# Attention with normalised queries and keys, then a bilinear FFN: queues ordered by a list, weights rounded in place, sums over keys by TensorE for 12 pairs

## The chip, the cores and the metric

The kernel runs on one core of a Trainium2 chip. The metric is the device time of one execution in microseconds, from the start of the program to its end; a span is the time from the first to the last instruction that the profiler recorded.

## The reference

Queries, keys and values are float32, of shape (8 batches, 12 heads, 448, 64). The weights of the FFN are float64: `w_a` and `w_b` 768 x 1536, `w_out` 1536 x 768.

```python
def rmsnorm(x, g):
    rms = np.sqrt(np.mean(x * x, axis=-1, keepdims=True) + 1e-06)
    return x / rms * g
q_n, k_n = (rmsnorm(q, g_q), rmsnorm(k, g_k))
scores = 1.0 / np.sqrt(64) * np.matmul(q_n, k_n.transpose(0, 1, 3, 2))
attn = np.exp(scores - np.max(scores, axis=-1, keepdims=True))
attn = attn / (np.sum(attn, axis=-1, keepdims=True) + 1e-09)
x = np.matmul(attn, v).transpose(0, 2, 1, 3).reshape(3584, 768)
out = ((x @ w_a) * (x @ w_b)) @ w_out
```

## The kernel before

All three rounded weights stay in SBUF. The work has three parts, which the program interleaves on in-order queues.

**Attention** goes by pairs of heads, 48 of them, six to a batch. `load` (line 149) brings a pair's queries, keys and values into two buffers each. `normalize` (164) squares q and k on POOL (172), sums on VectorE (173), raises the means to -0.5 with a power on POOL (176), and scales q on VectorE (179); the keys' scale goes into the exponential later. `transpose_qk` (185) makes eight transposes on TensorE into one PSUM tile and copies the halves out, k by ScalarE (197) and q with the gains by VectorE (198). `scores` (202) handles one of four key chunks of 112 for both heads: two products (207), two exponentials on ScalarE (211). `add_up` (213) adds the four chunks' exponentials, the first two on VectorE (217), then two additions of 112 x 896 on POOL (219). `values` (221) multiplies with v (227). `put_out` (256) copies the result into `xT`, the FFN's input, and `divide` (265) sums over the partitions with a product by ones that spreads the sum to 64 partitions per head (`su`, 270), takes a reciprocal of 128 x 448 (272) and multiplies `xT` (275). A pair's key sums thus use VectorE, POOL and TensorE in turn.

**Weights.** The float64 weights come in 72 units of 128 x 384: 48 of `w_a` and `w_b` in turn, by groups of 384 columns, then 24 of `w_out`. `load_weights` (115) brings a unit's words into one of two staging tiles (`raw`, low and high words side by side). `round_weights` (122) makes float32 of them: ScalarE (138) takes the high word's magnitude into `mag`, VectorE works in four steps (139 to 142), ScalarE scales the low word into `low` (143), and POOL multiplies and adds (144, 145). `mag` and `low` have one buffer each.

**The FFN** goes by eight blocks of 384 or 512 tokens (`ffn`, 277). The first stage has 12 column groups of 128; each takes six products with `w_a` and six with `w_b` into one of two PSUM tiles (`pf`, 285); ScalarE copies the first into `hT` (288), VectorE multiplies the second in (290). The second stage multiplies `hT` with `w_out` (`po`, 298) in two halves of 384 columns for each 128 tokens, copies out by VectorE or ScalarE (303, 305) and stores.

**The order** of the queues is the order in which the code issues. The main loop (344 to 382) goes by half pairs; `ffn` is a generator, and `some` (322) draws from it in proportion to the time of its products, so that a block's products are spread evenly over the six pairs of the next batch. Units are rounded one per half pair for the first 12 and six per half pair after that, all at one place of the loop (377 to 381). After the last pair the last block runs alone.

Of the kernel before, what the change touches and what calls it, by code (L numbers as in the profile page):

```python
# [22 lines left out]
ABOVE, BELOW = _float_of(0x47F00000), _float_of(0x38000000)  # L23


@with_exitstack
def kernel(
# [25 lines left out]
    nc = tc.nc  # L53
# [58 lines left out]
    def fast_body(ld, wk, ps_s, ps_o, ps_mm):  # L112
        raws = {}

        def load_weights(n):
            if n < len(units):
                src, dst, kc, c = units[n]
                raws[n] = ld.tile([P, WC, 2], U32, tag="stage", name="raw")
                nc.sync.dma_start(raws[n].rearrange("p n w -> p (n w)"),
                                  src[kc * P:(kc + 1) * P, 2 * c * WC:2 * (c + 1) * WC])  # L120

        def round_weights(n):

            if n >= len(units):
                return
            src, dst, kc, c = units[n]  # L130
            raw = raws.pop(n)
            lo, hi = raw[:, :, 0], raw[:, :, 1]
            w = dst[:, kc, c * WC:(c + 1) * WC]
            wb = w.bitcast(U32)
# [12 lines left out]
        qs, ks, vs, rs, qns, qkTs = {}, {}, {}, {}, {}, {}  # L147

        def load(p, what):
            if p >= NP:  # L150
                return
            b, h0 = p // HP, 2 * (p % HP)
            for held, src, nm in ((qs, q, "q"), (ks, k, "k"), (vs, v, "v")):
                if nm not in what:
                    continue
                if nm == "k":
                    held[p] = ld.tile([SP, NJ, 2, D], FP32, tag=nm, name=nm + "_sb")
                    for e in range(2):
                        nc.sync.dma_start(held[p][:, :, e], src[b, h0 + e].rearrange("(p j) d -> p j d", j=NJ))
                else:  # L160
                    held[p] = ld.tile([SP, 2, NJ * D], FP32, tag=nm, name=nm + "_sb")
                    nc.sync.dma_start(held[p], src[b, h0:h0 + 2].rearrange("h (p j) d -> p h (j d)", j=NJ))

        def normalize(p):

            if p >= NP:
                return
            ms = wk.tile([SP, 2, 2 * NJ], FP32, tag="ms", name="ms", bufs=3)
            for s, x in enumerate((qs[p], ks[p])):
                sq = wk.tile([SP, 2 * NJ, D], FP32, tag="sq", name="sq")  # L170
                flat = x.rearrange("p h (j d) -> p (h j) d", d=D) if s == 0 else x.rearrange("p j h d -> p (j h) d")
                nc.gpsimd.tensor_tensor(sq, flat, flat, ALU.mult)  # L172
                nc.vector.tensor_reduce(ms[:, s], sq, AX, ALU.add)  # L173
# [326 lines left out]
```

## Time and profile before

| | |
|---|---|
| median of 3 runs | 2007.9 us (2006.7 to 2008.88) |
| the profiled execution, its own time | 2006.51 us |
| its span | 2004.6 us |
| TensorE (PE) busy | 1769.9 us, 88% |
| VectorE (DVE), ScalarE (ACT), POOL busy | 594.9, 404.9 and 590.6 us |
| mean granted TensorE clock | 0.946 |

Busy time is the time in which an engine had an instruction running; PE is products, PEld the loading of stationary operands, which overlaps them. A granted clock of 1.00 is 2.4 GHz, 0.50 is 1.2 GHz. A float32 product leaves two records in the trace, a transpose one. The idle time of a row is that of the engine just ahead of its instructions, with what ended it. The rows are named by the line of the kernel and by tiles: `sc` scores, `ET` exponentials, `o` values' result, `pt` and `qkT` transposes and their copies, `ms` the means and the power, `su` and `sum` key sums, `pf` and `po` the FFN's two stages.

### The profile page before, as it was taken

The numbers are of one execution on the slowest core, as the hardware profiler recorded it, in microseconds if no ns is written. First come the engines' busy times: TensorE is split into PE (matmuls) and PEld (weight loads), VectorE is DVE, ScalarE is ACT, GpSimd is POOL, SyncE is SP. The second block draws the span as 40 slices with busy tenths as digits, with TensorE's granted clock in tenths as the row PEclk, the third lists the DMA queues.
The fourth block names the chain that finished last, engine by engine and source line by source line (L and its number), as shares of the span: only waits on it lengthen the run. The fifth ranks groups of instructions, "written<-read, shape, count | busy, mean of one in ns | idle before, by whom it ended". The sixth has DMA issues, their size and how long they took to land.

```text
span 2004.6 us, 15250 instructions
## 1 busy us (share of the span) xinstructions
PE 1769.9 (88%) x5760; PEld 851.6 (42%) x5760; DVE 594.9 (30%) x824; ACT 404.9 (20%) x773; POOL 590.6 (29%) x396
## 2 busy tenths in 40 slices
PE   4642455649999999999999999999999999999998
PEld 1211232324444455555444455554444555554445
DVE  4766544443223212232222122323222213210000
ACT  3423222322211112211121112121121112200000
POOL 5665544453212212322222123223212322200000
PEclk9885777779999999999999999999999999999999
DMA  3323223230100011001000111011010111000000
GB/s 90 80 66 102 80 76 92 78 93 22 39 19 14 18 34 36 25 17 44 22 14 14 39 34 28 14 35 30 14 28 14 30 30 28 5 16 8 0 6 27
DMA packets 87318, 73.43 MB, mean 37 GB/s; under 512 B 49348, under 2 KB 78020, under 8 KB 87236
## 3 DMA queue, kind: packets, MB, share of 16 engines
q1 hardware_dynamic: 87236, 72.38, 13.1%
q8 instruction: 47, 0.77, 0.2%
q14 instruction: 35, 0.29, 0.1%
HBM read 61.34 MB, written 11.01 MB: 36 GB/s over the span
## 4 chain that ended last, share of the span: by engine, by line
PE 80%; DVE 9%; POOL 7%; ACT 2%; issue 1%; SPq 0%; DMA 0%; POOLq 0%; DVEq 0%; ACTq 0%
PE pf L285 42%; PE po L298 22%; PE sc L207 6%; PE o L227 6%; POOL low L144 3%; PE su L270 2%; DVE mag L139 2%; POOL ms L176 2%; DVE sum L272 1%; POOL sum L219 1%; DVE mag L140 1%; ACT mag L138 1%; DVE mag L142 1%; PE pt L196 1%; PE pt L193 1%
## 5 line engine op out<-in xcount | busy, mean ns | idle before, releaser
L285 PE MATMUL pf<-xT,w_b_sb 128*128 128x512 f32 (+1 forms) x1152 | 460.4, 550 | 58.5 <-DVE hT L290 39.6
L285 PE MATMUL pf<-xT,w_a_sb 128*128 128x512 f32 (+1 forms) x1152 | 461.8, 551 | 43.1 <-ACT hT L288 43.1
L298 PE MATMUL po<-w_out_sb,hT 128*128 128x384 f32 x1344 | 446.7, 489 | 0.0
L285 PEld LDWEIGHTS pf<-xT,w_b_sb 128*128 128x128 f32 x1152 | 216.9, 192 | 294.7 <-issue 167.2
L298 PEld LDWEIGHTS po<-w_out_sb,hT 128*128 128x128 f32 x1344 | 251.2, 190 | 191.9 <-issue 28.4
L285 PEld LDWEIGHTS pf<-xT,w_a_sb 128*128 128x128 f32 x1152 | 218.8, 194 | 261.6 <-issue 152.6
L172 POOL TENSOR_TENSOR sq<-k_sb 112x512 f32<-112x512 f32 x48 | 49.9, 1040 | 852.7 <-DVE ms L173 852.7
L211 ACT ACTIVATE ET<-sc,ms 112x448 f32<-112x448 f32 x384 | 212.4, 637 | 243.8 <-PE sc L207 240.9
L219 POOL TENSOR_TENSOR sum<-sum,ET 112x896 f32<-112x896 f32 x96 | 200.0, 2084 | 130.4 <-ACT ET L211 79.2
L272 DVE RECIPROCAL sum<-su 128x448 f32<-128x448 f32 x48 | 141.9, 2957 | 270.8 <-PE su L270 270.8
L290 DVE TENSOR_TENSOR hT<-hT,pf 128x384 f32<-128x384 f32 (+1 forms) x96 | 59.4, 619 | 513.4 <-PE pf L285 513.0
L227 PE MATMUL o<-ET,v_sb 112*64 112x448 f32 x768 | 180.8, 594 | 19.2 <-ACT ET L211 19.2
L207 PE MATMUL sc<-qkT 64*112 64x448 f32 x768 | 173.6, 571 | 1.3 <-DVE qkT L198 1.3
L176 POOL TENSOR_TENSOR ms<-ms,expo 112x16 f32<-112x16 f32 x48 | 139.7, 2911 | 48.4 <-DVE ms L175 48.4
L288 ACT COPY hT<-pf 128x384 f32<-128x384 f32 (+1 forms) x96 | 51.1, 532 | 498.2 <-PE pf L285 498.2
L144 POOL TENSOR_TENSOR low<-low,mag 128x384 f32<-128x384 f32 x72 | 76.9, 1069 | 132.9 <-DVE mag L142 110.9
L207 PEld LDWEIGHTS sc<-qkT 64*112 64x112 f32 x768 | 62.6, 177 | 114.8 <-issue 103.1
L227 PEld LDWEIGHTS o<-ET,v_sb 112*64 112x64 f32 x768 | 50.6, 144 | 124.6 <-issue 98.7
L303 DVE COPY o_sb<-po 128x384 f32<-128x384 f32 x28 | 15.6, 557 | 228.6 <-PE po L298 228.6
L173 DVE TENSOR_REDUCE ms<-sq 112x8 f32<-112x512 f32 x96 | 65.5, 682 | 56.5 <-POOL sq L172 56.5
L138 ACT ACTIVATE mag<-raw 128x384 f32<-128x384 f32 x72 | 39.8, 553 | 192.4 <-POOL low L144 192.4
L179 DVE TENSOR_TENSOR qn<-q_sb,ms 112x512 f32<-112x512 f32 x48 | 34.0, 709 | 145.1 <-POOL ms L176 145.1
(42 smaller groups left out, 689.2 us busy)
## 6 DMA issues: line engine op xcount, KB each, us to landing
q_sb<-in_q_dram SPq DMA_DIRECT2D x48, 224.0 KB, 3.1
k_sb<-in_k_dram SPq DMA_DIRECT2D x96, 112.0 KB, 3.2
v_sb<-in_v_dram SPq DMA_DIRECT2D x48, 224.0 KB, 3.0
raw<-in_moe_w_a_dram SPq DMA_DIRECT2D x24, 384.0 KB, 3.2
raw<-in_moe_w_b_dram SPq DMA_DIRECT2D x24, 384.0 KB, 3.2
raw<-in_moe_w_out_dram SPq DMA_DIRECT2D x24, 384.0 KB, 3.0
out_dram<-o_sb SPq DMA_DIRECT2D x16, 168.0 KB, 2.1
out_dram<-o_sb SPq DMA_DIRECT2D x16, 144.0 KB, 2.0
```

The source lines that it names most:

```text
L138: nc.scalar.activation(magf, hi.bitcast(FP32), AF.Abs)
L144: nc.gpsimd.tensor_tensor(low, low, magf, ALU.mult)
L173: nc.vector.tensor_reduce(ms[:, s], sq, AX, ALU.add)
L176: nc.gpsimd.tensor_tensor(msf, msf, expo, ALU.pow)
L207: nc.tensor.matmul(sc[:, e, 0:S], lhsT=kT[rows, c * SP:(c + 1) * SP], rhs=qT[rows, :], start=True, stop=True)
L211: nc.scalar.activation(E[:, e], sc[:, e, 0:S], AF.Exp, scale=rs[p][:, 1, 2 * c + e:2 * c + e + 1])
L219: nc.gpsimd.tensor_tensor(sums[p][0:SP], sums[p][0:SP], ETs[p, c], ALU.add)
L227: nc.tensor.matmul(os_[p][e * D:(e + 1) * D, :], lhsT=vs[p][:, e, c * D:(c + 1) * D], rhs=E[:, e], start=(c == 0), stop=(c == NJ - 1))
L272: nc.vector.reciprocal(rinv, su)
L285: nc.tensor.matmul(pf[:, 0:N], lhsT=w_sb[:, c, m * P:(m + 1) * P], rhs=xT[:, c, 0:N], start=(c == 0), stop=(c == KA - 1))
L290: nc.vector.tensor_tensor(hT[:, m, 0:N], hT[:, m, 0:N], pf[:, 0:N], ALU.mult)
L298: nc.tensor.matmul(po[:, 0:HALF], lhsT=hT[:, m, t * P:(t + 1) * P], rhs=w_out_sb[:, m, hs], start=(m == 0), stop=(m == KO - 1))
```

## The change

**A planner.** Nothing is issued while the code walks the work. Each operation is put into a list with its engine, an assumed time, a key and the names of what it reads and writes, rings of buffers included (`Plan.op`, `Plan.slot`). `Plan.run` then goes through the list as a schedule at build time: at each step it takes the engine that can start first, and on it, among the operations ready at nearly the same time, the one of the smallest key. A chain of TensorE operations is kept together, and a change of TensorE's tiling costs 0.18 in it. The order so found is issued. A pair's operations have its number as key, a unit n/4 + 1, FFN products 10,000 and more, evacuations -1. FFN products are cut into groups of three (first stage) and six (second stage).

**Weights.** The rounding works in the weight's own place in place of `mag` and `low`, and in the staged words: the fourth VectorE step writes over the high words, the low word's product over the low words. The 48 units of `w_a` and `w_b` are staged in the twelve rows of `w_out`, whose own units come last and use two staging tiles as before. In every third unit one VectorE step replaces ScalarE's scaling and POOL's product.

**Pairs 0 to 11** (`LEAD`) sum over keys on TensorE alone: 32 products of a 112 x 112 piece of exponentials with one column of ones give the sums by query; VectorE inverts 112 x 8 numbers; eight products with the identity bring them to the layout of `xT`. VectorE's and POOL's additions are gone for these pairs. Their squares go from POOL to ScalarE, and the scaling of q's transposes from VectorE to ScalarE. Later pairs keep the old way, with the reciprocal written into PSUM. Squares now go k before q.

```diff
+class Plan:
...
+    def op(self, engine, us, key, emit, reads=(), writes=(), mode=None, chain=None, kb=0):
...
+        while any(cands.values()):
+            best = None
+            for e, cs in cands.items():
+                if not cs:
+                    continue
+                f = free.get(e, 0.0) if e else 0.0
+                at = {}
+                for n in cs:
+                    turn = self.TURN if ops[n][5] != modes.get(e) else 0.0
+                    at[n] = max(f, ready[n]) + turn
+                t = min(at.values())
+                n = min((n for n in cs if at[n] <= t + (0.2 if e == "PE" else 0.05)), key=lambda n: (ops[n][2], n))
+                if best is None or at[n] < best[0]:
+                    best = at[n], e, n
+            t, e, n = best
+            cands[e].remove(n)
+            for x in links.get(ops[n][6], [n]) if ops[n][6] is not None else [n]:
+                if ops[x][5] != modes.get(e) and x != n:
+                    t += self.TURN
+                modes[e] = ops[x][5]
+                order.append((t, x))
+                t += ops[x][1]
...
+                if ops[x][7]:
+                    dma = max(dma, t) + ops[x][7] / 200.0
+                    end[x] = dma + 2.5
...
+        self.times = order, end
+        for _, n in order:
+            if ops[n][3] is not None:
+                ops[n][3]()
...
+        LEAD = 12
...
+        def weights(n):
...
+            src, dst, kc, c = units[n]
+            key = n / 4 + 1.0
+            w = dst[:, kc, c * WC:(c + 1) * WC]
+            wb, hold = w.bitcast(U32), {}
+            if dst is w_out_sb:
+                st, name = slot("stage", 2), f"out.{kc}"
+            else:
+                st, name = f"out.{n % KO}", f"{'a' if dst is w_a_sb else 'b'}.{c}.{kc}"
...
+            def load():
+                if dst is w_out_sb:
+                    raw = ld.tile([P, WC, 2], U32, tag="stage", name="raw")
+                else:
+                    raw = w_out_sb[:, n % KO].bitcast(U32).rearrange("p (n w) -> p n w", w=2)
+                hold["lo"], hold["hi"] = raw[:, :, 0], raw[:, :, 1]
...
-            mag = wk.tile([P, WC], U32, tag="mag", name="mag")
-            low = wk.tile([P, WC], FP32, tag="low", name="low")
-            magf = mag.bitcast(FP32)
-            nc.scalar.activation(magf, hi.bitcast(FP32), AF.Abs)
-            nc.vector.tensor_scalar(magf, magf, BELOW, ABOVE, ALU.max, ALU.min)
-            nc.vector.tensor_scalar(mag, mag, 3, 0x3FFFFFFF, ALU.logical_shift_left, ALU.bitwise_and)
-            nc.vector.scalar_tensor_tensor(wb, hi, 0xC0000000, mag, ALU.bitwise_and, ALU.bitwise_or)
-            nc.vector.tensor_scalar(mag, wb, 0xFF800000, None, ALU.bitwise_and)
-            nc.scalar.activation(low, lo, AF.Copy, scale=2.0 ** -52)
-            nc.gpsimd.tensor_tensor(low, low, magf, ALU.mult)
-            nc.gpsimd.tensor_tensor(w, w, low, ALU.add)
...
+            op("SP", 0.1, key - 2.0, load, writes=[st], kb=384)
+            op("ACT", 0.55, key, lambda: nc.scalar.activation(w, hif(), AF.Abs), [st], [name])
+            op("DVE", 0.4, key, lambda: nc.vector.tensor_scalar(w, w, BELOW, ABOVE, ALU.max, ALU.min), [], [name])
+            op("DVE", 0.4, key, lambda: nc.vector.tensor_scalar(
+                wb, wb, 3, 0x3FFFFFFF, ALU.logical_shift_left, ALU.bitwise_and), [], [name])
+            op("DVE", 0.56, key, lambda: nc.vector.scalar_tensor_tensor(
+                wb, hold["hi"], 0xC0000000, wb, ALU.bitwise_and, ALU.bitwise_or), [st], [name])
+            op("DVE", 0.56, key, lambda: nc.vector.tensor_scalar(
+                hold["hi"], wb, 0xFF800000, None, ALU.bitwise_and), [name], [st])
+            if n % 3 == 0:
+                op("DVE", 0.56, key, lambda: nc.vector.scalar_tensor_tensor(
+                    lof(), hold["lo"], 2.0 ** -52, hif(), ALU.mult, ALU.mult), [], [st])
+            else:
+                op("ACT", 0.55, key, lambda: nc.scalar.activation(lof(), hold["lo"], AF.Copy, scale=2.0 ** -52), [], [st])
+                op("POOL", 1.05, key, lambda: nc.gpsimd.tensor_tensor(lof(), lof(), hif(), ALU.mult), [], [st])
+            op("POOL", 1.05, key, lambda: nc.gpsimd.tensor_tensor(w, w, lof(), ALU.add), [st], [name])
...
+                    if p < LEAD:
+                        nc.scalar.activation(t, flat, AF.Square)
+                    else:
+                        nc.gpsimd.tensor_tensor(t, flat, flat, ALU.mult)
...
+                if p < LEAD:
+                    nc.scalar.activation(qkTs[p][:, 0], x, AF.Copy, scale=gain[:, 0:1])
+                else:
+                    nc.vector.tensor_scalar_mul(qkTs[p][:, 0], x, gain[:, 0:1])
...
+            def by_query():
+                sus[p] = ps_o.tile([P, S], FP32, tag="su", name="su")
+                for e in range(2):
+                    for j in range(NJ):
+                        for c in range(NJ):
+                            nc.tensor.matmul(sus[p][0:SP, e * NJ + j:e * NJ + j + 1],
+                                             lhsT=ETs[p, c][:, e, j * SP:(j + 1) * SP], rhs=ones[:, 0:1],
+                                             start=(c == 0), stop=(c == NJ - 1))
...
+                rs["inv", p] = wk.tile([SP, 2 * NJ], FP32, tag="inv", name="inv", bufs=2)
+                nc.vector.reciprocal(rs["inv", p], sus[p][0:SP, 0:2 * NJ])
...
+            def to_features():
+                for e in range(2):
+                    for j in range(NJ):
+                        n = e * NJ + j
+                        nc.tensor.matmul(sus[p][e * D:(e + 1) * D, j * SP:(j + 1) * SP],
+                                         lhsT=rs["inv", p][:, n:n + 1].to_broadcast([SP, D]),
+                                         rhs=ident[0:SP, 0:SP], start=True, stop=True)
+            if p < LEAD:
+                inv = slot("inv", 2)
+                op("PE", 3.2, p, by_query, [names["ET", p, c] for c in range(NJ)], [su], mode="full", chain=chains[0])
+                op("DVE", 0.2, p - 1, invert_few, [su], [inv])
+                op("PE", 0.9, p, to_features, [inv], [su], mode="cols", chain=chains[1])
+            else:
+                op("PE", 0.76, p, spread, [names["sum", p]], [su], mode="cols", chain=chains[1])
+                op("DVE", 3.0, p, invert, [], [su])
...
+                        def products(m=m, n=n, w_sb=w_sb, part=part, cs=cs):
+                            if part == 0:
+                                pfs[m, n] = ps_mm.tile([P, 512], FP32, tag="mm", name="pf")
+                            for c in cs:
+                                nc.tensor.matmul(pfs[m, n][:, 0:N], lhsT=w_sb[:, c, m * P:(m + 1) * P],
+                                                 rhs=xTs[b][:, c, 0:N], start=(c == 0), stop=(c == KA - 1))
+                        op("PE", len(cs) * N / 600, key, products,
+                           [f"{names['xT', b]}.{c}" for c in range(KA)] + [f"{w}.{m * P // WC}.{c}" for c in cs],
+                           [mm], mode="full")
...
+        for n in range(len(units)):
+            weights(n)
...
+                    loads(p, nm)
+                normalize(p)
+                transposes(p)
+            if p > 0:
+                values(p - 1, 2, f"A{p}")
+                values(p - 1, 3, f"A{p}")
+                if p - 1 < LEAD:
+                    sums_over_keys(p - 1, (f"A{p}", f"B{p}"))
...
+            if p > 0:
+                if p - 1 >= LEAD:
+                    sums_over_keys(p - 1, (f"A{p}", f"B{p}"))
+                put_out(p - 1)
...
+            if p >= 2 * HP and p % HP == 0:
+                ffn(p // HP - 2)
+        ffn(B - 1)
...
-            load(1, "qk")
-            for n in range(2):
-                load_weights(n)
-            normalize(0)
-            transpose_qk(0)
-            todo, loaded = 0, 2
-            for i in range(NH + LAG):
-                p, h = divmod(i, 2)
...
-                if h == 0:
...
-                        divide(p - 1)
...
-                upto = i + 1 if i < 12 else 12 + (i - 11) * 6
-                while todo < min(upto, len(units)):
-                    load_weights(loaded)
-                    loaded += 1
-                    round_weights(todo)
-                    todo += 1
...
+            plan.run()
```

**How instructions move.** *TensorE, one pair in the first batch.* Before, from the transposes of pair 1 to its scores:

```order
L193 MATMUL pt<-ident,k_sb 128x112 x4
L196 MATMUL pt<-ident,qn 128x112 x4
L227 MATMUL o<-ET,v_sb 64x448 x4
L207 MATMUL sc<-qkT 112x448 x4
L270 MATMUL su<-sum,ones 64x448 x2
L227 MATMUL o<-ET,v_sb 64x448 x4
L207 MATMUL sc<-qkT 112x448 x4
```

and now, from the transposes of pair 2:

```order
L331 MATMUL pt<-ident,k_sb 128x112 x4
L331 MATMUL pt<-ident,qn 128x112 x4
L376 MATMUL o<-ET,v_sb 64x448 x4
L416 MATMUL su<-ones,ET 112x1 x32
L357 MATMUL sc<-qkT 112x448 x4
L428 MATMUL su<-ident,inv 64x112 x8
L376 MATMUL o<-ET,v_sb 64x448 x4
L357 MATMUL sc<-qkT 112x448 x4
```

The spread sum of two products became 32 products ahead of the next pair's scores (`su<-ones,ET`) and eight behind them (`su<-ident,inv`), and the inverse on VectorE now lies between these two.

*VectorE around the first evacuation into hT.* Before (30 units of weights stand ahead of it):

```order
L139 TENSOR_SCALAR mag<-mag 128x384
L140 TENSOR_SCALAR mag<-mag 128x384
L141 SCALAR_TENSOR_TENSOR w_b_sb<-raw,mag 128x384
L142 TENSOR_SCALAR mag<-w_b_sb 128x384
L217 TENSOR_TENSOR sum<-ET 112x896
L290 TENSOR_TENSOR hT<-hT,pf 128x384
L198 TENSOR_SCALAR qkT<-pt,gain 128x448
L139 TENSOR_SCALAR mag<-mag 128x384
L140 TENSOR_SCALAR mag<-mag 128x384
```

and now (49 stand ahead of it):

```order
L242 TENSOR_SCALAR w_out_sb<-w_out_sb 128x384
L243 TENSOR_SCALAR w_out_sb<-w_out_sb 128x384
L245 SCALAR_TENSOR_TENSOR w_out_sb<-raw,w_out_sb 128x384
L247 TENSOR_SCALAR raw<-w_out_sb 128x384
L250 SCALAR_TENSOR_TENSOR raw<-raw 128x384
L521 TENSOR_TENSOR hT<-hT,pf 128x384
L314 TENSOR_TENSOR qn<-q_sb,ms 112x2x4x64
L242 TENSOR_SCALAR w_out_sb<-w_out_sb 128x384
```

The evacuation moved behind all of `w_a` and `w_b`, and the inverse of pair 7 follows behind 50 units; the units are no longer in blocks of six.

*TensorE in a second stage of the FFN.* Before:

```order
L196 MATMUL pt<-ident,qn 128x112 x4
L298 MATMUL po<-w_out_sb,hT 128x384 x12
L227 MATMUL o<-ET,v_sb 64x448 x4
L207 MATMUL sc<-qkT 112x448 x4
L298 MATMUL po<-w_out_sb,hT 128x384 x12
L270 MATMUL su<-sum,ones 64x448 x2
L298 MATMUL po<-w_out_sb,hT 128x384 x12
L227 MATMUL o<-ET,v_sb 64x448 x4
L207 MATMUL sc<-qkT 112x448 x4
L298 MATMUL po<-w_out_sb,hT 128x384 x12
```

and now:

```order
L534 MATMUL po<-w_out_sb,hT 128x384 x6
L406 MATMUL su<-sum,ones 64x448 x2
L376 MATMUL o<-ET,v_sb 64x448 x4
L357 MATMUL sc<-qkT 112x448 x4
L534 MATMUL po<-w_out_sb,hT 128x384 x6
L331 MATMUL pt<-ident,k_sb 128x112 x4
L331 MATMUL pt<-ident,qn 128x112 x4
L534 MATMUL po<-w_out_sb,hT 128x384 x6
L376 MATMUL o<-ET,v_sb 64x448 x4
L357 MATMUL sc<-qkT 112x448 x4
```

A pair's pieces moved from 12 second-stage products apart to six, in the second stage and in the first groups of the next block; the rest of a first stage runs without pairs between.

## Rows read from the trace of the kernel before

**Rows 1.** Stretches: busy us (instructions) per engine, clock, DMA share, GB/s.
```profile
0.00:100.00 100.00, 56.15 (x209) 20.59 (x210) 61.87 (x78) 36.72 (x71) 62.01 (x48) 0.86 0.31 85
100.00:466.00 366.00, 181.03 (x596) 86.91 (x596) 195.10 (x328) 108.56 (x209) 198.26 (x166) 0.74 0.30 80
466.00:1900.00 1434.00, 1434.00 (x4681) 691.66 (x4680) 332.99 (x411) 255.35 (x487) 330.33 (x183) 1.00 0.09 24
```

**Rows 2.** Timeline: start us, us, engine, line, operation. VectorE, then TensorE.
```profile
15.48 1.52 DVE L179 TENSOR_TENSOR qn<-q_sb,ms 112x512 f32<-112x512 f32 x1 [3.03 <-POOL ms L176]
...
466.08 8.01 PE L298 MATMUL po<-w_out_sb,hT 128*128 128x384 f32 x24
```

**Rows 3.** TensorE's waits, 20 to 460 us: us in total, times, longest.
```profile
PE pf L285 <- ACT hT L288: 62.0, 5, 18.9
...
PE pf L285 <- DVE hT L290: 39.6, 2, 19.8
...
PE su L270 <- POOL sum L219: 17.2, 7, 3.3
```

**Rows 4.** Timeline, 204 to 213 us: one weight unit, and the next one's start.
```profile
208.02 0.55 ACT L138 ACTIVATE mag<-raw 128x384 f32<-128x384 f32 x1 [10.51 <-POOL low L144]
208.06 0.99 POOL L145 TENSOR_TENSOR w_a_sb<-w_a_sb,low 128x384 f32<-128x384 f32 x1
208.60 0.67 DVE L139 TENSOR_SCALAR mag<-mag 128x384 f32<-128x384 f32 x1 [1.76 <-ACT mag L138]
...
209.31 0.36 DVE L140 TENSOR_SCALAR mag<-mag 128x384 uint32<-128x384 uint32 x1
209.70 0.56 DVE L141 SCALAR_TENSOR_TENSOR w_b_sb<-raw,mag 128x384 uint32<-128x384 uint32 x1
210.29 0.36 DVE L142 TENSOR_SCALAR mag<-w_b_sb 128x384 uint32<-128x384 uint32 x1
...
211.82 0.55 ACT L138 ACTIVATE mag<-raw 128x384 f32<-128x384 f32 x1 [2.19 <-POOL low L144]
```

**Rows 5.** Timeline, 45 to 56 us: VectorE and POOL at the same time.
```profile
50.45 4.34 POOL L219 TENSOR_TENSOR sum<-sum,ET 112x896 f32<-112x896 f32 x2
...
50.75 2.12 DVE L140 TENSOR_SCALAR mag<-mag 128x384 uint32<-128x384 uint32 x1
...
52.90 2.31 DVE L141 SCALAR_TENSOR_TENSOR w_b_sb<-raw,mag 128x384 uint32<-128x384 uint32 x1
```

**Rows 6.** TensorE's groups by shape, 500 to 1900 us: busy us, mean ns, idle.
```profile
L298 PE MATMUL po<-w_out_sb,hT 128*128 128x384 f32 x1076 | 359.0, 490 | 0.0
...
L285 PE MATMUL pf<-xT,w_b_sb 128*128 128x384 f32 x432 | 147.7, 492 | 0.0
L207 PE MATMUL sc<-qkT 64*112 64x448 f32 x560 | 123.3, 559 | 0.0
L227 PE MATMUL o<-ET,v_sb 112*64 112x448 f32 x568 | 122.4, 552 | 0.0
...
L193 PE MATMUL pt<-ident,k_sb 112*128 112x112 f32 x140 | 19.2, 259 | 0.0
```

**Rows 7.** Timeline around 702 us: eight transposes, and what follows them.
```profile
701.65 0.55 PE L193 MATMUL pt<-ident,k_sb 112*128 112x112 f32 x4
...
702.42 7.92 PE L298 MATMUL po<-w_out_sb,hT 128*128 128x384 f32 x24
```

**Rows 8.** Line 207, 160 to 200 us: duration in ns, min/median/max.
```profile
L207 PEld LDWEIGHTS sc<-qkT x16: 169/173/308, 172.1 to 199.7; 64*112 64x112 f32 x16
```

**Rows 9.** Stretches as in rows 1: clock and TensorE's busy time.
```profile
48.00:52.00 4.00, 4.00 (x12) 1.28 (x10) 3.08 (x4) 1.60 (x4) 3.92 (x3) 0.50 0.32 98
```

**Rows 10.** The fullest stretch; two groups of the page.
```profile
36.00:40.00 4.00, 4.00 (x16) 1.20 (x12) 3.90 (x4) 1.28 (x3) 2.54 (x3) 0.64 0.99 265
...
L211 ACT ACTIVATE ET<-sc,ms 112x448 f32<-112x448 f32 x384 | 212.4, 637 | 243.8 <-PE sc L207 240.9
...
L176 POOL TENSOR_TENSOR ms<-ms,expo 112x16 f32<-112x16 f32 x48 | 139.7, 2911 | 48.4 <-DVE ms L175 48.4
```

More of the change, by code (lines that the diff above doesn't have):

```diff
@@ L152, in load, with loads, emit @@
+        xs, rs, qns, qkTs, pts, scs, ETs, sums, sus, os_, xTs, tails = ({} for _ in range(12))
+        names = {}
+        def loads(p, nm):
             b, h0 = p // HP, 2 * (p % HP)
-            for held, src, nm in ((qs, q, "q"), (ks, k, "k"), (vs, v, "v")):
-                if nm not in what:
-                    continue
+            src = {"q": q, "k": k, "v": v}[nm]
+            names[nm, p] = slot(nm, 2)
+            def emit():
                 if nm == "k":
-                    held[p] = ld.tile([SP, NJ, 2, D], FP32, tag=nm, name=nm + "_sb")
+                    x = ld.tile([SP, NJ, 2, D], FP32, tag=nm, name=nm + "_sb")
@@ L164, in normalize @@
+                    nc.sync.dma_start(x, src[b, h0:h0 + 2].rearrange("h (p j) d -> p h (j d)", j=NJ))
+                xs[nm, p] = x
+            op("SP", 0.15, p - 2.0, emit, writes=[names[nm, p]], kb=230)
         def normalize(p):
[L166 to L173, printed above, removed]
@@ L200, in fast_body @@
-        ETs, sums, os_, xTs, tails = {}, {}, {}, {}, {}
-        def scores(p, c):
-            qT, kT = qkTs[p][:, 0], qkTs[p][:, 1]
-            sc = ps_s.tile([SP, 2, 512], FP32, tag="sc", name="sc")
-            for e in range(2):
-                rows = slice(e * D, (e + 1) * D)
-                nc.tensor.matmul(sc[:, e, 0:S], lhsT=kT[rows, c * SP:(c + 1) * SP], rhs=qT[rows, :],
-                                 start=True, stop=True)
-            E = ETs[p, c] = wk.tile([SP, 2, S], FP32, tag="ET", name="ET", bufs=4)
-            for e in range(2):
-                nc.scalar.activation(E[:, e], sc[:, e, 0:S], AF.Exp, scale=rs[p][:, 1, 2 * c + e:2 * c + e + 1])
+            ms = names["ms", p] = slot("ms", 3)
@@ new lines, in values, with product @@
+        def values(p, c, chain):
+            if c == 0:
+                names["o", p] = slot("o", 1)
+            def product():
+                if c == 0:
+                    os_[p] = ps_o.tile([P, S], FP32, tag="o", name="o")
+                for e in range(2):
+                    nc.tensor.matmul(os_[p][e * D:(e + 1) * D, :], lhsT=xs["v", p][:, e, c * D:(c + 1) * D],
+                                     rhs=ETs[p, c][:, e], start=(c == 0), stop=(c == NJ - 1))
+            op("PE", 0.76, p, product, [names["ET", p, c], names["v", p]], [names["o", p]], mode="cols", chain=chain)
@@ L233, in fast_body, with emit @@
-        ends = []
-        for b in range(B):
-            ends.append((b + 1) * S // P * P)
+                names["sum", p] = slot("sum", 1)
+            def emit():
+                if c == 1:
+                    sums[p] = wk.tile([P, 2, S], FP32, tag="sum", name="sum")
+                    nc.vector.tensor_tensor(sums[p][0:SP], ETs[p, 0], ETs[p, 1], ALU.add)
+                else:
+                    nc.gpsimd.tensor_tensor(sums[p][0:SP], sums[p][0:SP], ETs[p, c], ALU.add)
+            E = names["ET", p, c]
@@ L316, in store @@
                 rows = out[bb * S:(bb + 1) * S].rearrange("(p j) d -> j p d", j=NJ)
-                nc.sync.dma_start(rows[j][p0:p0 + n, hs], o_sb[at:at + n])
+                nc.sync.dma_start(rows[j][p0:p0 + n, h * HALF:(h + 1) * HALF], o_sb[at:at + n])
                 g, at = g + n, at + n
-        fill, due, done = None, 0.0, 0.0
-        def some(share):
-            nonlocal fill, due, done
-            due += share
-            while fill is not None and done < due:
-                took = next(fill, None)
-                if took is None:
-                    fill = None
-                else:
-                    done += took
@@ L383, in fast_body @@
-            some(1e9)
-            fill, due, done = ffn(B - 1), 0.0, 0.0
-            some(1e9)
+            plan.run()
+        return plan
     def general():
```

360 lines of the change are left out of this document (220 added, 140 removed).

## The prediction

> **What bounds the kernel now.** I read the table of stretches first. It splits the run in two: up to 466 us TensorE is busy 56.15 of 100 and 181.03 of 366 us, at a mean granted clock of 0.86 and 0.74; from 466 to 1900 us it is busy 1434.00 of 1434.00 us at 1.00 [rows 1]. The cut is where TensorE issues its first product with the third weight, at 466.08 us [rows 2]. So whatever the change does, the time can come only from ahead of that point, and what follows it is 2004.6 - 466.1 = 1538.5 us of work that waits for nothing.
>
> Then the waits of TensorE ahead of that point: the first FFN block waits 62.0 us for ScalarE and 39.6 us for VectorE to take its results out of PSUM [rows 3]. Neither engine is short of time (VectorE is busy 195 of 366 us [rows 1]); they are waiting in order behind weight rounding. One unit is a chain, ScalarE at 208.02, VectorE from 208.60 to 210.65, then POOL, and the next unit's ScalarE step starts at 211.82, since it reuses the one `mag` tile: 3.80 us a unit [rows 4]. Six units stand between two hT evacuations. This chain is what the change goes at.
>
> **The sum.** Time = T0 + what TensorE does after its first third-weight product + 1.9 us (the profiled execution took 2006.51 us for a span of 2004.6; the median of the runs shown is 2007.9, 1.4 us more). T0 is 466.1 us before.
>
> **After T0.** At that point the new queue has issued 108 score, 104 value and 112 transpose products against 96, 92 and 96 before. Products count two records each, transposes one. A record is a group's busy time over its count [rows 6]: 24 x 0.220 + 24 x 0.2155 + 16 x 0.137 = 12.6 us; since neighbours overlap, the ten groups of that stretch add up to 1449 us in 1400, 3.5% too much, so 12.2 us. What remains is 1538.5 - 12.2 = 1526 us. The later order I cost at nothing: a pair's pieces are now 12 third-weight records (12 x 0.334 = 4.0 us) apart instead of 24, and that covers the hop that each piece waits for, the two exponentials of a chunk (2 x 0.64 us [rows 10]). POOL's two additions of 2.17 us [rows 5] have three such gaps. If the cover fails it is the spread sum that is late; that is a rival below.
>
> **T0, first part: to the reciprocal of pair 7.** On VectorE the first hT evacuation now stands behind 49 units, and the reciprocal of pair 7 behind 50, so the pace of units sets this part. In place, with 14 staging places, the chain across ScalarE is gone, and units overlap. What does not overlap is VectorE with POOL. VectorE's first step takes 0.67 us, ending 0.22 us after the POOL product beside it [rows 4], and where POOL adds 896 columns, VectorE's second step takes 2.12 us and its third 2.31 us, ending 0.42 us after POOL [rows 5]. Alone these are 0.36 and 0.56 [rows 4]. So I add what the two engines hold. A unit: POOL 1.67 products (two, one in every third unit) x 0.99 [rows 4] = 1.65; VectorE 4.33 steps, 1.67 of them behind POOL at 0.28 = 0.47, the other 2.67 at their own pitch of 0.45 (starts 209.31, 209.70, 210.29) = 1.20. Together 3.3 us; 50 units are 165 us. Nine pairs add POOL's power of 2.91 us [rows 10] and 0.5 of VectorE: 31 us. No row shows a VectorE step of this kind beside the power; it is worth 0 to 26 us, and I take all 26, since every other POOL row holds VectorE for its length. A start of 16 us (the first queries are normalised from 15.48 us on before [rows 2], behind the same loads and power) and 10 us, a twentieth, for a queue order that doesn't fit give 222 us.
>
> The Trainium skill, "SBUF — State Buffer", section "Who interferes with whom", has the pair of ports that VectorE and POOL share as a lock held for the whole instruction, which makes the unit 1.83 + 1.67 = 3.5 us (an estimate by that page) and T0 10 us later. The rows differ: the part outside the lock (0.36 against 0.22) does overlap, so the sum goes by the rows.
>
> The fourth step now writes every other word; 0.36 us if that is free, 0.56 if it costs what the strided third step does, at most 10 us here: taken as 0.36. Under this part lie ScalarE (a step of 0.55 [rows 4] and two thirds of another per unit, per pair 8 exponentials of 0.64 and six steps like these: some 120 us) and the transfers (50 units of 393 KB and ten pairs of 0.69 MB, 27 MB; at the 265 GB/s of the fullest stretch [rows 10], 100 us).
>
> **T0, second part: TensorE.** All of TensorE's work before T0 at full clock: scores 13.5 pairs x 16 x 0.220, values 13 x 16 x 0.2155, transposes 14 x 8 x 0.137, 288 first-stage records x 0.342, together 206, less the 3.5%: 199 us [rows 6]. New are the sums by query: 32 products, 64 records, each loading 112 columns to move one. No row has that. Eight transposes, which load 128 columns and move 112 each, take 0.77 us, 0.096 each [rows 7]; 112/240 of that, 0.045, is the floor if time goes by columns, and the ceiling is the 0.173 us (median) that loading 112 columns for a score takes when nothing hides it [rows 8]. I take 0.07, nearer the transposes: 4.5 us a pair, and 1.2 us for the 16 records that bring the inverse back: 12 x 5.7 = 68 us. The spread sums of these pairs are not in the 199. Total 267 us; up to the sums of pair 7 it is 118 us, under the 222 above; 149 us remain. I add 12 us (8%) for waits and low clock: from 48 to 52 us TensorE was busy throughout and the clock granted was 0.50, the lower level of 1.2 GHz [rows 9]. T0 = 222 + 149 + 12 = 383 us. In this part the last 22 units have two staging tiles, as before, where a unit took 3.80 us [rows 4]: 84 us, or 110 at 5 us; they lie under it.
>
> The Trainium skill, "TensorE: Matmul & The Clock Gate", section "LDWEIGHTS (loading the stationary operand)", gives columns over 1.2 as ns: 93 ns for 112 columns, so 6 us a pair (an estimate by that page) and a sum 6 us higher; no run shows a load with nothing to hide it at full clock.
>
> VectorE's additions and long reciprocals and POOL's additions leave twelve pairs: worth nothing beyond the pace above, which already lacks them. What is late next is TensorE itself.
>
> **Forecast:** 383 + 1526 + 2 = 1911 us. Half of the chances; own range 1870 to 1945.
>
> **Rivals.**
> - VectorE and POOL hide under TensorE after all (the power holds nothing, the planner's order fits): T0 = 16 + 267 + 27 (a tenth for waits) = 310, 1838 us. For: 3.3 us is the pace only if both engines always have work. Against: the 2.12 us step. Chance 0.18.
> - The sums by query cost their load's whole 0.173: 12 x 12.3 = 147 in place of 68, and TensorE bounds all along: T0 = 16 + 199 + 147 + 42 of waits (a fifth of the 199) = 404, 1932 us. For: it is what a load of 112 columns takes. Against: the transposes' 0.096. Chance 0.15.
> - A new wait later: pairs bunched at 20 us instead of 33 make TensorE wait for POOL's sums 17.2/7 = 2.5 us each [rows 3] for 36 pairs: +88, 1999 us. Against: three gaps of 4 us. Chance 0.09.
> - Slower: the sums by query run at the longest load of [rows 8], 0.308 us, because the clock falls while they move one column each: 12 x 20.9 = 251, T0 = 16 + 199 + 251 + 42 = 508, 2036 us. It decides from 0.27 us a record, where T0 passes 478. For: the clock in [rows 9]. Against: of 16 loads in that row the median is 0.173. Chance 0.05.
> - Nothing moves, since something I don't see (the loads' order on the sync queue, which now waits for a place in the third weight's home) holds units at their old 3.8 us: about the time before. The queue rows show the change does what it says. Chance 0.03.
>
> **Numbers.** A measurement of this kernel tells 0.2% (4 us) from no change. Faster 0.5 + 0.18 + 0.15 + 0.09 = 0.92, same 0.03, slower 0.05. The range goes from just under the PE-bound case to between the two dearer ones: 1830 to 1970 us; outside lie most of the bunching case, the slower one and the tails.
>
> **What would show it.** In the profile after: first third-weight product at 383 us; VectorE's first two steps at 0.5 to 0.7 us in the mean beside POOL; TensorE waiting for VectorE (hT, inverse) until about 222 us and hardly after; the sums by query at 4 to 5 us a pair; from T0 on TensorE busy all the time. It is wrong if the sums by query fill 10 us a pair, if VectorE's steps run at 0.36 beside POOL, or if TensorE waits after T0.

## The result, and the profile after

The changed kernel takes 1896.06 us (median of 4 runs, 1895.93 to 1896.3) against 2007.3 us before: a ratio of 0.9445, 95% interval 0.9429 to 0.9461, faster by 111 us. The forecast was 1911 us, its own range 1870 to 1945, the range over all rivals 1830 to 1970.

TensorE's first product with the third weight now starts at 379.7 us (466.08 before [rows 2]; forecast 383). The stretches up to it and behind it, with columns as in [rows 1]:

```profile
0.00:100.00 100.00, 68.79 (x363) 46.56 (x364) 71.17 (x134) 45.66 (x91) 50.98 (x49) 0.75 0.60 181
100.00:379.70 279.70, 278.17 (x1424) 180.71 (x1423) 153.54 (x290) 110.91 (x219) 128.01 (x107) 0.86 0.27 77
379.70:1894.20 1514.50, 1506.88 (x4889) 745.39 (x4887) 352.33 (x401) 249.67 (x476) 309.61 (x169) 1.00 0.08 22
```

Of the 111 us, 86.4 lie ahead of that product and 24 behind it (1538.5 before, 1514.5 now); the forecast had 83 and 12. So far it is near the forecast. But from 100 us on TensorE is busy 278 of 280 us, at a granted clock of 0.86: the engine that was to wait for VectorE until 222 us does not wait. All its waits from 60 to 379 us are one row:

```profile
PE pt L331 <- ACT ET L363: 2.0, 4, 0.5
```

What it does instead shows in the timeline (TensorE: start, us, operation; the sums of pair 1, then a whole turn from pair 2's sums on), and in stretches: the sums of pair 1, and for pair 6 the sums by query and the scores behind them (columns as above; the clock is the third number from the end). The stretch of pair 6's sums leaves out their edges; the timeline has 8.86 us for them.

```profile
63.41 12.11 PE L416 MATMUL su<-ones,ET 112*112 112x1 f32 x64
...
87.76 8.48 PE L416 MATMUL su<-ones,ET 112*112 112x1 f32 x64
96.17 3.33 PE L357 MATMUL sc<-qkT 64*112 64x448 f32 x8
99.43 2.00 PE L428 MATMUL su<-ident,inv 112*64 112x112 f32 x13
...
101.78 1.80 PE L376 MATMUL o<-ET,v_sb 112*64 112x448 f32 x7
103.52 1.76 PE L357 MATMUL sc<-qkT 64*112 64x448 f32 x8
```

```profile
63.50:75.50 12.00, 12.00 (x66) 11.98 (x66) 5.32 (x9) 1.91 (x5) 7.00 (x5) 0.50 0.18 66
173.60:182.20 8.60, 8.60 (x64) 8.60 (x64) 5.81 (x11) 2.75 (x5) 4.64 (x3) 0.71 0.09 30
182.40:185.50 3.10, 3.10 (x8) 0.97 (x8) 3.02 (x7) 1.16 (x2) 2.04 (x1) 0.50 0.00 0
```

While TensorE sums by query its records leave no gap, and yet the clock falls, to 0.71 in the mean of this stretch and to 0.50 (1.2 GHz) in the scores behind it. Those eight records take 3.33 us; the pair's other eight, at full clock, take 1.76. The sums of pair 1 ran at 0.50 from end to end and took 12.11 us; the other eleven pairs took 7.8 to 8.9. From one pair's sums to the next's (108.36) TensorE needs 20.6 us, 8.5 of them for sums that the prediction had at 4.5.

### The profile page after: what moved, and what is told of

The parts are those of the page before. It is cut to its first block, busy times and chain, and to the rows that moved or that the text cites. A ratio compares the mean times of both kernels' runs of the same rounds, so it can differ in the third digit from the quotient of the medians.

```text
span 1894.2 us, 16866 instructions
## 1 busy us (share of the span) xinstructions
PE 1853.9 (98%) x6672; PEld 972.7 (51%) x6672; DVE 577.0 (30%) x824; ACT 406.2 (21%) x785; POOL 488.6 (26%) x324
## 4 chain that ended last, share of the span: by engine, by line
PE 97%; DVE 1%; SPq 0%; ACT 0%; POOL 0%; DMA 0%; issue 0%; POOLq 0%; DVEq 0%; ACTq 0%
PE pf L510 46%; PE po L534 23%; PE sc L357 9%; PE o L376 8%; PE su L416 5%; PE pt L331 2%; PE su L406 2%; PE su L428 1%; ACT ET L363 0%; DMA w_out_sb<-in_moe_w_a_dram 0%; POOL sum L390 0%; POOL ms L310 0%; DVE su L409 0%; DVE w_a_sb L245 0%; DVE w_out_sb L247 0%
## 5 line engine op out<-in xcount | busy, mean ns | idle before, releaser
L510 PE MATMUL pf<-xT,w_b_sb 128*128 128x512 f32 (+1 forms) x1152 | 453.7, 542 | 0.0
L510 PE MATMUL pf<-xT,w_a_sb 128*128 128x512 f32 (+1 forms) x1152 | 453.1, 541 | 0.0
L534 PE MATMUL po<-w_out_sb,hT 128*128 128x384 f32 x1344 | 453.1, 490 | 0.0
L534 PEld LDWEIGHTS po<-w_out_sb,hT 128*128 128x128 f32 x1344 | 249.1, 190 | 192.5 <-issue 35.9
L390 POOL TENSOR_TENSOR sum<-sum,ET 112x896 f32<-112x896 f32 x72 | 152.6, 2119 | 442.7 <-DVE sum L388 303.2
L357 PE MATMUL sc<-qkT 64*112 64x448 f32 x768 | 189.0, 615 | 1.2 <-ACT qkT L341 1.2
L376 PE MATMUL o<-ET,v_sb 112*64 112x448 f32 x768 | 171.9, 556 | 0.0
L409 DVE RECIPROCAL su<-su 128x448 f32<-128x448 f32 x36 | 106.8, 2967 | 122.2 <-PE su L406 122.2
L416 PEld LDWEIGHTS su<-ones,ET 112*112 112x112 f32 x768 | 103.7, 229 | 9.1 <-PE o L376 3.5
L416 PE MATMUL su<-ones,ET 112*112 112x1 f32 x768 | 104.7, 273 | 0.0
L314 DVE TENSOR_TENSOR qn<-q_sb,ms 112x512 f32<-112x512 f32 x48 | 62.9, 1310 | 85.0 <-issue 65.3
```

What stands on the lines that cost most here:

```text
L314: nc.vector.tensor_tensor(qns[p].rearrange("p j h d -> p h j d"), xs["q", p].rearrange("p h (j d) -> p h j d", d=D), rs[p][:, 0].rearrange ...
L357: nc.tensor.matmul(t[:, e, 0:S], lhsT=qkTs[p][rows, 1, c * SP:(c + 1) * SP], rhs=qkTs[p][rows, 0, :], start=True, stop=True)
L376: nc.tensor.matmul(os_[p][e * D:(e + 1) * D, :], lhsT=xs["v", p][:, e, c * D:(c + 1) * D], rhs=ETs[p, c][:, e], start=(c == 0), stop=(c == ...
L390: nc.gpsimd.tensor_tensor(sums[p][0:SP], sums[p][0:SP], ETs[p, c], ALU.add)
L409: nc.vector.reciprocal(sus[p], sus[p])
L416: nc.tensor.matmul(sus[p][0:SP, e * NJ + j:e * NJ + j + 1], lhsT=ETs[p, c][:, e, j * SP:(j + 1) * SP], rhs=ones[:, 0:1], start=(c == 0), s ...
```

## The experiments

All times are medians; the kernel before took 2007 to 2009 us beside each of them. `LEAD` = 0 is order, rule, rounding in place and staging together.

| kernel | us | | kernel | us |
|---|---|---|---|---|
| before | 2007.3 | | **change** | **1896.1** |
| before, units spread evenly | 2017.9 | | change, old staging and chain | 1905.3 |
| order alone | 1931.4 | | 56 columns of ones | 1860.2 |
| order, rule for every third unit | 1924.0 | | a quarter of the sums | 1834.5 |
| order, rule, rounding in place | 1934.3 | | eight products with ones | 1837.5 |
| order, rule, third weight's home | 1923.9 | | the same, 16 pairs | 1831.4 |
| `LEAD` = 0 | 1910.8 | | the same, four pairs by query | 1854.5 |

### What do the sums by query cost?

**56 columns.** The same loads, the same number of products, the same queue order; each product moves more:

```diff
-  rhs=ones[:, 0:1],
+  rhs=ones[:, 0:56],
```

> Each of the 32 products of the sums by query moves 56 columns of ones in place of one (same result, written 56 times). If a load's own time sets the pace of these records (0.12 to 0.14 us each in the change, whatever is moved): no change, 1896 us within 4. If the clock falls because they move so little: the clock granted in the scores behind them is 1.00 in place of 0.50 (1.76 us for the first four scores, not 3.33), the sums themselves run in 4.5 to 6 us in place of 8.6, and the time falls by 12 x 3 to 5 = 36 to 60 us, to 1835 to 1860 us. If they cost by what they move: up to 0.05 us a record more, 12 x 3.2 = 38 us, 1935 us. Pace theory: no change (at most plus or minus 10 us).

1860.2 us (two runs, 1857.6 and 1862.9), 36 us faster (ratio to before 0.9265, interval 0.9247 to 0.9284), though each product moves 56 times as much. Timeline and stretches of one pair:

```profile
78.29 6.50 PE L416 MATMUL su<-ones,ET 112*112 112x56 f32 x64
84.72 1.76 PE L357 MATMUL sc<-qkT 64*112 64x448 f32 x8
```

```profile
78.40:84.60 6.20, 6.20 (x64) 6.20 (x64) 5.92 (x11) 2.73 (x7) 2.90 (x3) 1.00 0.77 208
84.80:86.40 1.60, 1.60 (x8) 0.55 (x8) 1.53 (x3) 0.00 (x0) 1.43 (x2) 1.00 0.72 207
```

The clock stays at 1.00, a record takes 6.50/64 = 0.102 us, and the scores behind are back at 1.76; all twelve pairs have these times. So it was the clock: the load's own pace is 0.102, and one column a product pushed it to 0.136 in the mean (104.7 us of TensorE for 768 records) and nearly doubled the next scores. The two other readings (no change; dearer by what is moved) fall. The gain lies at the lower edge of the 36 to 60 us expected, since the sums still take 6.5 us where 4.5 to 6 was expected.

**A quarter of the sums.**

```diff
-  for c in range(NJ):
+  for c in (0,):
```

> The sums by query take one of four key chunks (8 products a pair in place of 32; the other three chunks are left out of the key sums). TensorE theory: 48 records a pair less at 0.13 us = 6.2 us, and the scores behind them back at full clock, 1.6 us: 12 x 6.2 to 7.8 = 75 to 94 us off T0 if VectorE can follow; it is busy 41 of 50 us up to 190 us, so it can be at most a fifth faster. T0 300 to 330, total 1815 to 1845 us. Pace theory: only the pairs behind pair 7 gain, at 0.07 us a record, 5 x 3.4 = 17 us: 1879 us.

1834.5 us, 62 us off and inside what the TensorE theory gave; the 17 us of the pace theory are out. This run also shows VectorE's pace when TensorE has less to do, and that it does bind then. VectorE is busy 96.68 of 100 us:

```profile
50.00:150.00 100.00, 66.02 (x348) 37.25 (x348) 96.68 (x170) 58.74 (x123) 69.69 (x57) 0.76 0.49 141
```

```profile
PE su L428 <- DVE inv L422: 26.4, 5, 7.6
```

The second row is TensorE's largest wait from 60 to 172 us; after that there is none but one of 0.3 us. In these 100 us VectorE finished 31 units and 6 pairs. By busy time its unit steps (lines 242 to 250) take 84.0 us, 2.7 a unit, and the pairs' steps 19.7, 3.3 a pair; neighbouring records overlap by 7 us in all. At the times that they take alone (0.36, and 0.56 for the third and the every-third step) the unit steps would take 56 us, so a third of a unit's price is time beside POOL.

**The part as a whole, left out.**

```diff
-  LEAD = 12
+  LEAD = 0
```

> LEAD = 0: every pair adds over keys on VectorE and POOL, squares on POOL, q scaled on VectorE; the queue order from the list, the rounding in place and the staging in the third weight's home stay. TensorE theory (the sums by query fill TensorE: 8 to 9 us a pair, and the scores behind them run at half clock): TensorE loses 12 x (8.6 + 1.6 + 2.0 - 1.0) = 134 us of work ahead of its first third-weight product, while VectorE gains 12 x 4.7 and POOL 12 x 6 us; these two then bound, T0 400 to 440, total 1915 to 1955 us. Pace theory (the prediction's: VectorE and POOL set T0 up to pair 7): 9 x (4.2 + 1.1 + 0.7) = 54 us more of them to pair 7, 68 us less of TensorE in all, T0 about 410, total 1925 us. Both: slower than the change by 1 to 3 per cent; the run prices the part, it does not tell the two apart by its time alone, but by whether TensorE waits.

1910.8 us (0.9516, 0.95 to 0.9532): 15 us slower than the change and 4 under the lower end of what the TensorE theory gave. So the sums for twelve pairs, with their squares and scaling, are worth 15 us as they are. But both theories had the first third-weight product at 400 us or later, and it comes at 350.3, 29 us ahead of the change's, behind as many scores, values and transposes; the loss lies behind it, 1559.1 us in place of 1514.5, with 36 us of TensorE's waits. Over the whole run TensorE waits for other tiles than in [rows 3]:

```profile
PE pt L331 <- DVE qn L314: 104.0, 14, 23.3
PE sc L357 <- DVE qkT L343: 30.1, 13, 6.5
```

**Another way to the same sums.** In the chain of a pair, in place of `by_query`, `invert_few` and `to_features`:

```diff
+  for c in range(NJ):
+      for e in range(2):
+          nc.tensor.matmul(sus[p][e * D:(e + 1) * D, :], lhsT=ones, rhs=ETs[p, c][:, e],
+                           start=(c == 0), stop=(c == NJ - 1))
...
+  nc.vector.reciprocal(sus[p], sus[p])
```

> Pairs 0 to 11 sum over keys on TensorE in another way: eight products of ones (112 x 64) with the 448 columns of exponentials, two to a chunk, added up in PSUM, which gives the sums spread over the features at once; VectorE's long reciprocal of 128 x 448 takes the place of the short one, the eight products with the identity go. TensorE theory: 16 records x 0.2155 = 3.45 us a pair in place of 8.6 + 2.0, and the clock stays at 1.00, which gives back 1.6 us of scores: 8.8 x 11 = 97 us off TensorE; VectorE gains 12 x 2.76 = 33 us and may bind. T0 300 to 340, total 1815 to 1855 us. Pace theory: T0 later by 8 x 2.76 = 22 us less 5 x 2 us = 12 us, total 1908 us.

1837.5 us (0.9153, 0.9137 to 0.9168), 59 us under the change. The sums take 3.18 us in nine pairs and 3.7 to 3.8 in three, and in none do the scores behind them slow down:

```profile
73.91 3.18 PE L412 MATMUL su<-ET,ones 112*64 112x448 f32 x16
77.02 1.76 PE L357 MATMUL sc<-qkT 64*112 64x448 f32 x8
```

From 300 to 350 us TensorE was busy only 38.38 of 50 us, so two more followed. Sixteen pairs this way (`LEAD = 16`):

> The eight products with ones for pairs 0 to 15 in place of 0 to 11. With LEAD = 12 TensorE idled 11.6 of 50 us from 300 to 350 us, where pairs 12 on add up on VectorE and POOL while the last units are still rounded. If that is the cause, the idle time goes and four pairs cost TensorE 2.6 us each more: 1825 to 1837 us (1837.5 with 12). If the idle time comes from the units alone: 1840 to 1850 us.

1831.4 us (5 runs, 1830.8 to 1831.6; 0.9118, 0.9105 to 0.913), as expected: the idle time is gone, and this is the fastest version of the study, 65 us under the change. The stretch with 12 pairs and with 16:

```profile
300.00:350.00 50.00, 38.38 (x162) 17.16 (x162) 38.89 (x45) 19.36 (x40) 26.83 (x19) 0.92 0.25 73
```

```profile
300.00:350.00 50.00, 50.00 (x201) 24.67 (x200) 23.30 (x41) 16.23 (x34) 18.33 (x16) 1.00 0.24 73
```

And with pairs 0, 2, 4 and 6 summed by query over 56 columns, to relieve VectorE:

> The same, but pairs 0, 2, 4 and 6 sum by query with 56 columns of ones (short reciprocal): VectorE, full until 200 us, loses 4 x 2.76 = 11 us, TensorE, idle 25 us from 50 to 200 us, gains 4 x 4.5 = 18 us. If VectorE sets the pace there: 8 to 11 us under the run beside it, 1815 to 1828 us. If TensorE's idle time can't be filled by these (they stand where it is busy): 5 to 10 us over it.

1854.5 us, 23 us over the run beside it, a miss worse than either reading. TensorE's idle time moved instead of going: its wait for q falls from 27.0 to 19.7 us, and one for the short inverse comes, 19.0 us in 4 (`PE su L435 <- DVE inv L429`). With ScalarE's waits, 10.3 us against 15.9, that is 6 us more idle time, and the 18 us of extra work on top.

### Which part carries the gain?

The prediction put the gain down to the chain through `mag`. These take the parts away from `LEAD` = 0, where VectorE is nearly always busy. Only staging in two tiles again (`slot("stage", 2)` for all units):

> LEAD = 0, and all 72 units staged in two tiles as before the change, in place of the third weight's home (rounding still in place, order from the list). Against the run with LEAD = 0 alone (1910.8 us), where VectorE is busy 48.8 of 50 us from 50 to 250 us. If VectorE is what sets the pace there, two staging tiles cover a load of 3.4 us and the time stays, 1905 to 1920 us. If the staging is what the change lives on: a unit holds its tile for its load, its chain and its queues, some 9 to 12 us, so two tiles give 4.5 to 6 us a unit against (264.4 - 12.3) / 48 = 5.25 us now: up to 48 x 0.75 = 36 us, 1947 us.

1934.3 us, 23 us slower, between the two. By the code, rounding in place holds a unit's staging tile up to POOL's last addition, since the fourth step and the product write into it. That two tiles are too few for that is argued from the code; the run shows the 23 us. Only one `mag` and one `low` again:

> LEAD = 0, and the rounding through one `mag` and one `low` tile as before the change, in place of working in the weight's own place (staging in the third weight's home, the every-third rule and the order from the list stay). VectorE theory: in the mean a unit comes every 5.25 us, the chain needs 3.80, the pair's own VectorE work fills the gaps if the list places it there: 1910 to 1930 us. Chain theory (the reason that I gave for the gain): VectorE idles 1.76 us a unit for ScalarE as before (rows 4), 48 x 1.76 = 84 us, of which the pairs' work takes back at most half: 1950 to 1995 us.

1923.9 us, 13 us slower, by the VectorE theory. Both:

> LEAD = 0, two staging tiles and one `mag` and `low`: what is left of the change is the order from the list (with FFN products in smaller groups, and the every-third rule). If the order alone carries most of the 97 us between before and LEAD = 0: 1910 to 1940 us. If rounding and staging carry it: 1970 to 2010 us.

1924.0 us (0.9581, 0.9565 to 0.9597). So staging and rounding in place give 13 us together; staging alone gives nothing, and rounding in place alone costs 10. Both taken from the change itself:

> The changed kernel (LEAD = 12) with two staging tiles and one `mag` and `low`: order and sums by query alone. TensorE theory: in the change TensorE is busy all the time from 60 us on but for small gaps, and VectorE only 41 of 50 us, so slower units cost little: 1890 to 1925 us. Pace theory (the prediction's: VectorE with POOL sets T0 up to pair 7): a unit at 3.80 us and the pairs' work on top in place of 3.3, and an idle 1.76 us for each: 50 x 0.5 to 1.8 = 25 to 90 us more, 1920 to 1985 us.

1905.3 us (0.949, 0.9474 to 0.9506): 9 us slower than the change, where the prediction's own pace asked for 25 at least. Even these 9 us don't lie where the prediction put the gain: the first third-weight product comes earlier than in the change, at 365.8 us, and behind it 1539.8 us remain in place of 1514.5. And, with `LEAD` = 0 again, the every-third rule taken out as well, so that of the change the list's order is left:

> LEAD = 0, two staging tiles, one `mag` and `low`, and now every unit with ScalarE's scaling and POOL's product as before the change: of the change only the order from the list is left (with its smaller FFN groups, k's squares ahead of q's and the reciprocal in PSUM). If the order carries the gain: 24 VectorE steps of 0.56 go and 24 POOL products of 0.83 come, each of which can hold VectorE; 1915 to 1935 us. If the rule for every third unit carried a part of the 84 us: 1940 to 1990 us.

1931.4 us (0.9621, 0.9605 to 0.9637). The order alone is worth 76 us, the rule 7. "Order" here includes the smaller FFN groups, k's squares ahead of q's and the reciprocal in PSUM, which no run takes apart. In the first 466 us VectorE is busy 366 us, 257 before (before, then order alone):

```profile
0.00:466.00 466.00, 237.19 (x804) 107.50 (x804) 256.96 (x405) 145.28 (x279) 260.26 (x214) 0.77 0.30 81
```

```profile
0.00:466.00 466.00, 307.69 (x1140) 135.93 (x1140) 366.24 (x460) 181.49 (x354) 334.89 (x245) 0.83 0.32 91
```

A part of that is not more work but longer steps. VectorE's second step (before, then order alone: busy us, mean ns) starts beside a running POOL instruction 8 times in 72 before and 54 times now, and takes twice as long in the mean:

```profile
L140 DVE TENSOR_SCALAR mag<-mag 128x384 uint32<-128x384 uint32 x72 | 40.0, 555 | 2.5
L256 DVE TENSOR_SCALAR mag<-mag 128x384 uint32<-128x384 uint32 x70 | 76.5, 1093 | 2.2
```

TensorE's waits for hT, 62.0 and 39.6 us in [rows 3], shrink to 0.6 and 1.8 us; the wait for q grows from 35.9 us to 103.4. VectorE's idle time behind ScalarE's magnitude falls from 92.1 us (`DVE mag L139 <- ACT mag L138`) to 60.9, with the same single `mag` (order alone):

```profile
PE pf L522 <- DVE hT L533: 1.8, 1, 1.8
PE pt L343 <- DVE qn L326: 103.4, 13, 21.4
```

```profile
DVE mag L255 <- ACT mag L245: 60.9, 43, 3.9
```

Is it just that units no longer come in sixes? The kernel before with one number changed:

```diff
-  upto = i + 1 if i < 12 else 12 + (i - 11) * 6
+  upto = 7 * (i + 1) // 2
```

> The kernel before, with one number changed: 3.5 units of weights per half pair from the start on, in place of one for the first twelve half pairs and six for each after that (nothing of the list, of the rounding in place, of the staging or of the sums by query). The order alone was worth 84 us in the run with LEAD = 0, two staging tiles and the chain. If that was the bunching of units in sixes (TensorE waited 101.6 us for evacuations into hT behind them, rows 3): half of it or more comes back with this number alone, 1925 to 1965 us. If it was the choice of the list from one operation to the next (an evacuation or a q scaling put ahead of units, FFN products in smaller groups): within 15 us of 2007.

2017.9 us (1.0045, 1.003 to 1.006): 9 us slower. TensorE's waits for hT do fall, to 30.7 us, and others take their place:

```profile
PE pt L193 <- ACT ET L211: 94.3, 8, 13.8
PE o L227 <- ACT ET L211: 81.8, 7, 12.0
PE pf L285 <- ACT hT L288: 17.7, 4, 7.5
PE pf L285 <- DVE hT L290: 13.0, 2, 8.4
```

Spreading the units evenly is not it. What is left is the choice from one operation to the next, which is shown as a whole and by elimination only: which of its choices (evacuations first, smaller FFN groups, a pair's work in the gaps of a unit) is worth how much was not tried.

## Why the prediction was right, and where it wasn't

The number was right by luck; two of its terms were wrong, in opposite directions. With TensorE alone binding, the prediction's own first rival has the first third-weight product at 310 us. Taking VectorE as the bound put 73 us on that; leaving out 80 us of TensorE's work took as much away.

**The bound, and where the time is.** Right: the time comes from ahead of 466 us and from the pieces done there. Their counts at the cut are as forecast (108 score, 104 value and 112 transpose products).

**"50 units are 165 us", 222 us to the reciprocal of pair 7.** Too long, and not what bound. In the quarter run VectorE needed 100 us for 31 units and 6 pairs; the prediction's terms give 31 x 3.3 + 6 x 3.4 = 123. Most of the difference is the unit, at 2.7 in place of 3.3. The pair came out near its price for the wrong reason: it takes 3.3 us of VectorE's own steps, where the prediction had 0.5 of these and, on top, the power, taken as holding VectorE for all of its 2.91 us. In the change the steps beside it (start, us) run as if alone, 0.35, 0.56 and 0.36:

```profile
97.16 0.35 DVE L243 TENSOR_SCALAR w_a_sb<-w_a_sb 128x384 uint32<-128x384 uint32 x1
97.33 2.95 POOL L310 TENSOR_TENSOR ms<-ms,expo 112x16 f32<-112x16 f32 x1 [1.24 <-DVE ms L306]
97.54 0.56 DVE L245 SCALAR_TENSOR_TENSOR w_a_sb<-w_out_sb,w_a_sb 128x384 uint32<-128x384 uint32 x1
98.14 0.36 DVE L247 TENSOR_SCALAR w_out_sb<-w_a_sb 128x384 uint32<-128x384 uint32 x1
```

Between the bounds of 0 and 26 us, the lower was near right: of the 57 steps beside the power alone 55 ran at their own time, two second steps took 0.87 and 1.06. Beside POOL's addition into the weight it is as in [rows 5]: the third step ends 0.42 us after POOL:

```profile
110.55 1.01 POOL L255 TENSOR_TENSOR w_b_sb<-w_b_sb,w_out_sb 128x384 f32<-128x384 f32 x1
110.72 1.26 DVE L245 SCALAR_TENSOR_TENSOR w_a_sb<-w_out_sb,w_a_sb 128x384 uint32<-128x384 uint32 x1
```

The first two steps average 0.36 and 0.70 us from 50 to 150 us, beside POOL or not, so 0.53, inside the 0.5 to 0.7 forecast. The Trainium skill, "SBUF — State Buffer", section "Who interferes with whom", says that whoever issues first has the shared pair of ports for the whole instruction; for POOL's addition the trace agrees but for 0.14 us (0.56 alone, 0.42 behind POOL), for the power it doesn't.

**"I take 0.07" for a record of the sums by query.** The step that failed most. Measured 104.7/768 = 0.136, of which 0.102 is the load at full clock (so the transposes' 0.096 was the right neighbour, without the fraction for columns) and the rest the clock. The forecast had a falling clock only in the slower rival, at 0.308. TensorE was busy 68.79 + 278.17 = 347 us ahead of the cut, not 267: by the pace of the records from 60 us on, the sums took 105 us in place of 54, the scores, half of them at half clock, 68 for 48, the inverse back 19 for 14. The Trainium skill, "TensorE: Matmul & The Clock Gate", section "LDWEIGHTS (loading the stationary operand)", gives 0.093 us for 112 columns; the run with 56 columns agrees within a tenth.

**222 + 149 + 12 = 383.** What happened is 347 us of work and 33 of idle time, 31 of it in the first 60 us. That is the mechanism of the rival at 1932 us, TensorE bounding all along, at 0.136 a record where it had 0.173. By the signs that the prediction set itself its mechanism was wrong: TensorE's waits for VectorE were over within the first 60 us, not at 222, and the sums took 8.7 us a pair in the mean, not 4 to 5; with the 1.6 that they cost the scores behind them that is the 10 at which it called itself wrong.

**"This chain is what the change goes at."** The weight was wrong. Taken away one after another, the sums for twelve pairs are worth 15 us, rounding in place and staging 13 (9 in the change itself), the rule 7, the order 76. VectorE's idle time behind ScalarE [rows 4] was read as the chain's; with the chain still there the order alone took 31 of its 92.1 us away and gave 76 of the 111.

**After the cut, "at nothing".** Right that nothing waits there (0.3 us), and the rival of bunched pairs falls. It is 11.5 us shorter than 1526. The 2,016 first-stage records behind the cut take 776.5 us from start to next start, 787.4 before the change. Most of that lies at the edges of uninterrupted stretches of such records, of which there are 29 in place of 97: inside a stretch a record takes 0.38 us in both, the first and the last of one together 0.13 more than two inside. With 68 stretches fewer that is 9 of the 10.9 us; the prediction costed the new order at nothing in this direction too.

## What to carry to other kernels

Here a product of one column cost its load, and the scores behind it ran at half clock: where a matrix of data would be loaded to multiply a single vector, load the vector (repeated) and move the data. When two engines might bind, work out both totals to the end; a forecast whose first engine is too dear and whose second too cheap can hit the number and mislead about what to mend next. Before a wait is put down to a dependence, ask what else stood ready in that queue.

## What the hardware showed that I had not expected

- TensorE's clock fell to 1.2 GHz while the profile has it busy without a gap (8.60 of 8.60 us in both its records and its loads), and stayed at 2.4 GHz when the same loads each moved 56 columns.
- POOL's power of 112 x 16, 2.9 us long, hardly slows VectorE's steps beside it (2 of 57 were slower): the third step, 0.56 alone and 1.25 beside POOL's addition, was 0.56 in all 16 cases beside the power alone.
- 64 loads of 112 x 112 took 7.8 to 12.1 us with one-column products and 6.5 with 56-column products; multiplying ones with the same exponentials took 3.2 to 3.8.
